# Score matmuls split around an mm1, one PSUM tile per bank and finer filling products in a recurrent attention with a cosine feed-forward layer

## The chip, the cores and the metric

The kernel runs on one core of a Trainium2 chip. The metric is the device time of one execution in microseconds (us), the median of several runs of the same program. The engines are TensorE (PE, with its weight loads listed as PEld), VectorE (DVE), ScalarE (ACT), GpSimd (POOL) and SyncE (SP), which here issues nearly all DMAs.

## The reference

Two parts follow each other: an attention with a decaying state, and a feed-forward layer whose gate is h*cos(h).

```
for t in range(S):                       # B=4, H=8, S=768, D=48
    cur = einsum('bhd,bhe->bhde', u[None] * kt, vt)
    y[:, :, t] = einsum('bhd,bhde->bhe', rt, state + cur)
    state = wt[:, :, :, None] * state + einsum('bhd,bhe->bhde', kt, vt)

x = y.transpose(0, 2, 1, 3).reshape(B * S, H * D)    # 3072 x 384
h = x @ w_in                                          # w_in 384 x 2048
g = h * cos(h)
out = g @ w_out                                       # w_out 2048 x 384
```

## The kernel before, in words

**Tiling.** The 3072 tokens are 24 chunks of 128; two chunks (`BLK`) make a block of 256 tokens, and there are 12 blocks. The hidden size 2048 is cut into 8 units of 256 for each block. A unit is one `mm1` (18 matmuls of 128x256, L594), a gate, and one `mm2` (12 matmuls of 128x384, L612). The factors are split into a high and a low fp32r part and multiplied in three passes (`PASSES`), so 18 is 2 tiles x 3 contractions x 3 passes. The gate of a unit has six steps: I (ACT, L557) and S (DVE, L560) reduce the argument, N (ACT, L573) is the sine, M (DVE, L574) multiplies by h, H (ACT) makes the high part `gs`, L (POOL) the low part. `mm2` of a unit is issued two units after its `mm1` (`LAG`). `mm1` writes its result `ph` into one of two PSUM banks in turn, so `mm1` of a unit writes the bank whose last reader is M of two units before.

**Attention of a chunk.** It is made one block ahead of its use, in small steps that stand between the gate's steps: e and f are scans that make the decays (L283, L289), r and k scale the factors (L300, L302), `lr`, `m`, `u`, `c` and A make `asb`, a tile with the bonus term on its diagonal (A on POOL, L335). `a` (function `att_scores`, L382) computes the scores of the chunk with 16 matmuls into two PSUM banks `pa`, and P (L396) places them into `asb` with six predicated copies on DVE. `t` turns the keys with 16 DMA transposes into `top0` or `top1` (L425, on SP), K brings them from there into `kn` (DVE, L429). `o`, `p` and `s` (matmuls into `py` and `pst`, L479 to L513 and L444) use `asb`, the state and `kn` to make the output and the next state; d makes the decayed state `dd` (DVE, L358).

**What sets the order.** The engines PE, DVE, ACT and POOL run their instructions in the order in which the program is written. `START` orders the first two blocks by hand, `FIRST` the third, and the eight rows of `PLAN`, one for each unit, the blocks after it; `LAST` is the end. In a row, `a+2` is step a of the chunk two after the block's first one, and the names I S N M mm2 H L are those of the unit itself, in the order of their issue; `up` (called by the rows) issues `mm1` and `mm2`. The order of SP's queue is made by a scheduler from when its DMAs' data are made and freed.

**Banks.** `bank(kind, shape, name)` takes the next PSUM bank of a kind by turns from `BANKS[stage]`; from the end of `START` (stage 3) kind a, for `pa`, `py`, `pst`, has the four banks a0, a1, a2, h2, and kind h, for `ph`, has h0 and h1. Each call makes a new tile there, and the program waits, at a tile's first use, until the one before it in that bank is done with.

**Filling products.** D in `START` (handled in `at_first`, L740) issues matmuls of the identity with itself into a bank that nobody reads, while PE has nothing else to do.

Of the kernel before, what the change touches and what calls it, by code (L numbers as in the profile page):

```python
# [10 lines left out]
F32 = mybir.dt.float32  # L11
# [11 lines left out]
C = 128  # L23
# [34 lines left out]
PLAN = ["mm1 I S k+3 N M mm2 H L f+3",  # L58
# [7 lines left out]
START = """  # L66
ld0 e0 f0 ld1 raw2 raw1 q0 e1 k0 D3 pc0 r0 q1 cd0 v0 v1 raw0 f1 D3 a0 W0 wg2 wl2 A0 k1 pc1 wl1 r1 wy2 P0 cd1 D1 a1
wc2 t0 wg1 A1 ld3 ld2 wg0 W1 t1 P1 v5 wx2 wy1 o0 K0 K1 xh0.0 xp0.0 s0 wl0 e3 q3 wc1 xa0.0 wy0 wc0 xh0.1 wp1 f3 pc3
xp0.1 wv1 wx0 xa0.1 q2 e2 n0 k3 f2 raw3 k2 m0.0 m1.0 pc2 t3 r3 I0 r2 wg3 raw4 v2 wl3 cd2 v3 raw5 wy3 m0.1 cd3 S0 t2 a3
A3 K3 K2 A2 P3 ld7 wl4 wg4 a2 ld5 wc3 wg5 N0 raw8 raw6 P2 s1 wx3 raw9 n1 o1 xh1.0 xl1.0 raw7 lr5 v4 ld4 m1.1 xh1.1  # L70
# [26 lines left out]
def rwkv_cos_ffn(ctx: ExitStack, tc: tile.TileContext, tr, tn, tv, u, ut, wts, w, rkw, vst, us, xs, out):  # L97
    nc = tc.nc
# [12 lines left out]
    ps = fast.enter_context(tc.tile_pool(name="ps", bufs=1, space=bass.MemoryType.PSUM))  # L111
    turn = {"a": 0, "h": 0}

    def bank(kind, shape, name):

        tags = BANKS[stage[0]]
        turn[kind] += 1
        return ps.tile(shape, F32, tag=tags[kind][turn[kind] % len(tags[kind])], name=name)

    stage = [0]  # L120

    def buf(tag, shape, dtype, name=None, pool=sb):
        return pool.tile(shape, dtype, tag=tag, name=name or tag, bufs=BUFS.get(tag, 1))
    ident = cst.tile([C, C], F32, name="ident")
# [51 lines left out]
    def fetch_weights(f):  # L176

        place = NF + 1 - RING + (f - 1) % RING
        raw[f] = wt.tile([128, 4 * DM], I32, tag=f"w{place}", name="raw")
        E["qf"].dma_start(out=raw[f].bitcast(I16)[:, :8 * DM - 1], in_=wts[f, :, 1:])  # L180
# [55 lines left out]
    def chunk(j):  # L236

        if j not in atts:
            atts[j] = {"j": j, "g": order[j], "b": order[j] // NCB, "c": order[j] % NCB}
        return atts[j]  # L240

    def att_load(j):
        a = chunk(j)
        g = a["g"]
        a["tt"] = tt = buf("tt", [C, TRW], F32)
        half = 1024 + NP // 2 * 129
        for cols in (*(((half, TRW), (1024, half)) if not atts_loaded else ((1024, TRW),)), (512, 1024), (0, 512)) if j < IN_PARTS else ((0, TRW),):
            E["qt"].dma_start(out=tt[:, slice(*cols)], in_=tr[g, :, slice(*cols)])  # L248
        a["tt"] = tt = tt[:R]
        a["r3"] = tt[:, 0:512].rearrange("p (a t) -> p a t", a=NP)  # L250
        a["k3"] = tt[:, 512:1024].rearrange("p (a t) -> p a t", a=NP)
        a["halves"] = not atts_loaded
        atts_loaded.append(j)
        if j == 0:
            E["qt"].dma_start(out=u_by_head, in_=ut)
# [51 lines left out]
    def att_diag(a):  # L307
        if a["j"] < BY_PE:
            pc = bank("a", [C, 512], "pc")[:, :8]
            for p in range(NP):  # L310
                nc.tensor.matmul(out=pc[:, 2 * p:2 * p + 2], lhsT=a["rkt"][:, p], rhs=u_by_head[:, p], start=True, stop=True)

            def sums():
                a["cd"] = buf("cd", [C, 8], F32)
                copy("cd", a["cd"], pc)

            part(("cd", a["j"]), sums)
        else:
            rk = a["rk"][:, 0]
            part(("m", a["j"]), lambda: E["rk"].tensor_tensor(out=rk, in0=rk, in1=a["rk"][:, 1], op=ALU.mult))  # L320
            part(("u", a["j"]), lambda: E["ru"].tensor_tensor(out=rk, in0=rk, in1=told["u"], op=ALU.mult))

            def sums():
                a["cd"] = buf("cd", [C, 8], F32)
                nc.vector.tensor_reduce(out=a["cd"], in_=rk.rearrange("p (h d) -> p h d", d=HD), axis=mybir.AxisListType.X, op=ALU.add)  # L325

            part(("c", a["j"]), sums)
        part(("A", a["j"]), lambda: picked(a))
# [22 lines left out]
    def att_dstate(a):  # L351

        if a["c"] == 0:
            return

        def decayed():
            a["dd"] = buf("dd", [R, NP, HD], F32)
            E["dd"].tensor_tensor(out=a["dd"], in0=states[a["b"]], in1=a["ee"][:, :, 0:1].to_broadcast([R, NP, HD]), op=ALU.mult)  # L358

        def placed():  # L360
            a["past"] = past[a["j"] % BLK]
            for h in range(2):
                copy("pc%d" % h, a["past"][rows(h), :, h * HD:(h + 1) * HD], a["dd"][rows(h)])

        part(("d", a["j"]), decayed)
        part(("pp", a["j"]), placed)
# [215 lines left out]
    def mm1(t, half=None):  # L582
        i, u = seq[t]
        if not half:
            for j in range(BLK):
                att(i * BLK + j, "x")
            units[t] = bank("h", [C, FU, BT], "ph")
        xT, ph = xts[i], units[t]
        for fi in range(FU) if half is None else (half,):
            steps_of = [(kt, a, b) for kt in range(KT) for a, b in PASSES]  # L590
            if half is not None:
                steps_of.sort(key=lambda x: (x[1], x[2]))
            for n, (kt, a, b) in enumerate(steps_of):
                nc.tensor.matmul(out=ph[:, fi], lhsT=wgt[u * FU + fi][:, 0, a, kt * 128:(kt + 1) * 128], rhs=xT[:, b, kt],  # L594
                                 start=n == 0, stop=n == 3 * KT - 1)
        if half is None or half == FU - 1:
            gate(sb, ph, t)
# [40 lines left out]
    for i in PAIR:  # L638
# [7 lines left out]
                 a=att_scores, t=att_transpose, s=att_state, o=att_own, p=att_past, x=att_x)  # L646
# [64 lines left out]
    def at_first(token):  # L711

        by = re.match(r"(W|H|wc)([av])(\d+)$", token)
        if by:
            name = dict(W="whole", H="gh", wc="whi0")[by[1]]
            usual, E[name] = E[name], dict(a=nc.scalar, v=nc.vector)[by[2]]
            parts.pop((by[1], int(by[3])))()
            E[name] = usual
            return
        if token[:2] == "wp":  # L720
            parts.pop(("wx", int(token[2:])))
        if token[:2] == "wx":
            for x in "wp", "wv":
                parts.pop((x, int(token[2:])))
        if token[:2] == "xp":
            parts.pop(("xl", (int(token[2]), int(token[4]))))
        if token[:2] == "xl":
            for x in "xp", "xa":
                parts.pop((x, (int(token[2]), int(token[4]))))
        n, at, side = re.match(r"(mm2\.|m[01]\.|[a-zA-Z]+)(\d+)(?:\.(\d))?$", token).groups()  # L730
        j = int(at)
        if n == "ld":
            att_load(j)
            att_decay(atts[j])
            seen.update({(j, "load"), (j, "decay"), (j, "x")})
        elif n == "D":
            tags = BANKS[stage[0]]["h"]
            filled = ps.tile([C, 4, C], F32, tag=tags[(turn["h"] + 1) % len(tags)], name="filled")
            for again in range(j):
                nc.tensor.matmul(out=filled, lhsT=ident, rhs=ident.unsqueeze(1).to_broadcast([C, 4, C]), start=True, stop=True)  # L740
        elif n == "raw":
            fetch_weights(j)
            load_weights(j)
        elif n in ("v", "lr"):
            steps[{"v": "lv", "lr": "lr"}[n]](chunk(j))
            seen.add((j, {"v": "lv", "lr": "lr"}[n]))
            if n == "lr":
                att_diag(chunk(j))
                seen.add((j, "diag"))
        elif n == "pc":  # L750
            att_diag(atts[j])
            seen.add((j, "diag"))
        elif n in ("a", "t"):
            steps[n](atts[j])
            seen.add((j, n))
        elif n in ("o", "p", "s"):
            steps[n](j)
            seen.add((j, n))
            if n == "o" and atts[j * BLK]["c"] == 0:
                att_past(j)  # L760
                seen.add((j, "p"))
        elif n in ("m0.", "m1."):
            mm1(j, int(n[1]))
        elif n == "mm2.":
            mm2(j)
        else:
            if n == "d":
                att_dstate(atts[j])
                seen.add((j, "d"))
            parts.pop((n, (j, int(side)) if side else j))()  # L770
            if n == "A" and j == ALL_OF - 1:
                nc.gpsimd.tensor_copy(out=turned_mask, in_=mask)
                nc.gpsimd.memset(turned_mask[:ROW, TURNED:, ROW:], 0)
                nc.gpsimd.memset(turned_mask[ROW:, TURNED:, :ROW], 1)
# [219 lines left out]
```

## Time and profile before

| | before |
|---|---|
| median of 3 runs | 497.48 us |
| lowest and highest run | 496.69, 498.38 us |
| the profiled execution, its own time | 497.93 us |
| its span | 496.1 us |
| mean granted TensorE clock | 0.998 |
| PE busy | 487.1 us |
| PEld busy | 466.8 us |
| DVE busy | 393.2 us |
| ACT busy | 257.8 us |
| POOL busy | 218.0 us |

The span is what the profiler saw of one execution, from the first to the last instruction; the execution's own time lies around it. Busy times are sums over an engine's instructions; weight loads overlap matmuls. In the chain and the waits, "issue" is time in which an engine waited for nothing that the profile shows. A matmul of fp32 factors is two records in the trace, so the 16 score matmuls of a chunk are 32 records, the scores of a block 64, and a filling product is two.

### The profile page before, as it was taken

The numbers are of one execution on the slowest core, as the hardware profiler recorded it, in microseconds if no ns is written. First come the engines' busy times: TensorE is split into PE (matmuls) and PEld (weight loads), VectorE is DVE, ScalarE is ACT, GpSimd is POOL, SyncE is SP. The second block draws the span as 40 slices with busy tenths as digits, with TensorE's granted clock in tenths as the row PEclk, the third lists the DMA queues.
The fourth block names the chain that finished last, engine by engine and source line by source line (L and its number), as shares of the span: only waits on it lengthen the run. The fifth ranks groups of instructions, "written<-read, shape, count | busy, mean of one in ns | idle before, by whom it ended". The sixth has DMA issues, their size and how long they took to land.

```text
span 496.1 us, 13443 instructions
## 1 busy us (share of the span) xinstructions
PE 487.1 (98%) x5514; PEld 466.8 (94%) x5514; DVE 393.2 (79%) x681; ACT 257.8 (52%) x444; POOL 218.0 (44%) x280
## 2 busy tenths in 40 slices
PE   8999999999999999999999999999999999999996
PEld 4689999999999999999999999999999999999996
DVE  7999899898979779769968958967966967587632
ACT  3899988435445445444445345345435445544542
POOL 5138798344436236234435343534624533432330
PEclk9999999999999999999999999999999999999999
DMA  8998830234444152153152150242223212023001
GB/s 275 416 400 296 345 107 6 49 110 130 125 127 158 20 199 80 18 199 77 19 201 49 45 191 22 80 120 96 75 67 133 65 32 97 33 68 127 32 2 36
DMA packets 46289, 58.59 MB, mean 118 GB/s; under 512 B 30736, under 2 KB 37392, under 8 KB 46224
## 3 DMA queue, kind: packets, MB, share of 16 engines
q1 hardware_dynamic: 46080, 57.59, 35.4%
q8 instruction: 45, 0.74, 0.6%
q14 instruction: 20, 0.16, 0.1%
q10 hardware_dynamic: 144, 0.10, 0.1%
HBM read 49.80 MB, written 4.72 MB: 110 GB/s over the span
## 4 chain that ended last, share of the span: by engine, by line
PE 89%; DVE 4%; DMA 2%; ACT 2%; SPq 1%; issue 1%; POOL 0%; DVEq 0%
PE ph L594 40%; PE acc L612 38%; PE pa L382 3%; PE py L479 2%; PE py L485 2%; DMA raw<-wts 2%; PE py L513 1%; PE pst L444 1%; DVE h L203 1%; PE py L507 1%; DVE rr L560 1%; DVE w L205 1%; SPq L248 1%; DMA rk<-tt 0%; PE pa L374 0%
## 5 line engine op out<-in xcount | busy, mean ns | idle before, releaser
L174 POOL TENSOR_TENSOR gs<-rr,gs 128x256 fp32r<-128x256 f32 x188 | 160.8, 876 | 217.9 <-ACT gs L171 209.7
L594 PE MATMUL ph<-xT,w 128*128 128x256 f32 x1728 | 219.7, 281 | 0.8 <-DVE rr L574 0.6
L594 PEld LDWEIGHTS ph<-xT,w 128*128 128x128 f32 x1728 | 212.3, 188 | 4.8 <-PE py L513 1.8
L612 PE MATMUL acc<-w,gs 128*128 128x384 f32 x1152 | 215.3, 337 | 0.1
L612 PEld LDWEIGHTS acc<-w,gs 128*128 128x128 f32 x1152 | 196.3, 188 | 0.7 <-ACT ob L626 0.4
L573 ACT ACTIVATE rr<-rr,quarter 128x512 f32<-128x512 f32 x96 | 69.5, 724 | 94.2 <-DVE rr L560 94.0
L560 DVE SCALAR_TENSOR_TENSOR rr<-rr,ph 128x512 f32<-128x512 int32 x96 | 65.5, 682 | 45.5 <-ACT rr L557 44.8
L171 ACT CAST gs<-rr 128x512 fp32r<-128x512 f32 x92 | 57.1, 621 | 69.0 <-DVE rr L574 48.9
L574 DVE TENSOR_TENSOR rr<-rr,ph 128x512 f32<-128x512 f32 x96 | 65.1, 679 | 21.8 <-ACT rr L573 19.4
L557 ACT ACTIVATE rr<-ph 128x512 int32<-128x512 f32 x96 | 57.1, 595 | 39.2 <-PE ph L594 38.7
L335 POOL TENSOR_SCALAR_AFFINE_SELECT asb<-cd 128x512 f32<-128x512 f32 x48 | 35.4, 762 | 45.4 <-DVE cd L325 27.0
L396 DVE COPY_PREDICATED asb<-turned_mask,pa 64x128 f32<-64x128 uint8 (+1 forms) x108 | 33.6, 346 | 2.1 <-POOL asb L335 0.3
L283 DVE TENSOR_TENSOR_SCAN ee<-tt,one_e 112x516 f32<-112x516 f32 (+1 forms) x25 | 32.7, 1312 | 1.9 <-DMA tt<-tr 1.9
L289 DVE TENSOR_TENSOR_SCAN tt<-tt,inj 112x516 f32<-112x516 f32 x24 | 30.3, 1261 | 0.8
L174 DVE TENSOR_TENSOR xT<-py,xT 128x384 fp32r<-128x384 f32 x22 | 11.3, 550 | 17.4 <-ACT xT L171 17.4
L195 ACT ACTIVATE top<-raw 128x768 f16<-128x768 bf16 x16 | 17.3, 1088 | 3.8 <-DMA raw<-wts 3.0
L479 PE MATMUL py<-asb,v 128*32 128x128 f32 x384 | 18.0, 276 | 0.3 <-DVE asb L393 0.2
L485 PE MATMUL py<-asb,v 128*32 128x128 f32 x384 | 17.3, 273 | 0.0
L171 ACT CAST xT<-py 128x384 fp32r<-128x384 f32 x24 | 10.5, 482 | 12.6 <-PE py L513 8.4
L203 DVE CUSTOM_DVE_ANT_0 h<-h,top 128x1536 uint16<-128x1536 uint16 x16 | 16.3, 1021 | 0.5 <-ACT h L191 0.5
L171 ACT COPY past<-dd 48x192 f32<-48x192 f32 x40 | 14.0, 349 | 2.7 <-DVE dd L358 2.4
L382 PEld LDWEIGHTS pa<-tt 48*64 48x64 f32 x576 | 12.9, 134 | 2.2 <-issue 2.2
(94 smaller groups left out, 352.9 us busy)
## 6 DMA issues: line engine op xcount, KB each, us to landing
tt<-tr SPq DMA_DIRECT2D x22, 770.5 KB, 7.0
raw<-wts SPq DMA_DIRECT2D x16, 767.8 KB, 6.6
rk<-tn SPq DMA_DIRECT2D x20, 384.0 KB, 4.2
v<-tv SPq DMA_DIRECT2D x24, 224.0 KB, 4.5
ww<-w SPq DMA_DIRECT2D x6, 768.0 KB, 5.3
out<-ob SPq DMA_DIRECT2D x23, 192.0 KB, 2.0
top<-tt SPq DMA_DIRECT2D x112, 16.0 KB, 1.9
top<-tt SPq DMA_DIRECT2D x112, 8.0 KB, 1.8
```

What stands on the lines that cost most here:

```text
L171: (nc.scalar.copy if E[name] is nc.scalar else E[name].tensor_copy)(out=out, in_=in_)
L174: E[name].tensor_tensor(out=out, in0=full, in1=high.bitcast(F32), op=ALU.subtract)
L283: nc.vector.tensor_tensor_scan(out=ee[:, pairs].rearrange("p a t -> p (a t)")[:, ::-1], data0=wp[:, cols][:, ::-1], data1=one_e[:, pairs]. ...
L289: nc.vector.tensor_tensor_scan(out=wp[:, 0:W129], data0=wp[:, 0:W129], data1=inj.rearrange("p a t -> p (a t)"), initial=0.0, op0=ALU.mult, ...
L335: nc.gpsimd.affine_select(out=asb, in_=col.unsqueeze(2).to_broadcast([C, NP, C]), pattern=[[0, 4], [1, C]], compare_op=ALU.is_equal, fill= ...
L396: nc.vector.copy_predicated(*(which(x) for x in (a["asb", h], turned_mask, pa[h])))
L557: nc.scalar.activation(made["rr"].bitcast(I32), ph, AF.Copy, scale=INV2PI / W_SCALE, bias=0.25)
L560: nc.vector.scalar_tensor_tensor(out=made["rr"], in0=made["rr"].bitcast(I32), scalar=-2.0 * math.pi * W_SCALE, in1=ph, op0=ALU.mult, op1=A ...
L573: N=lambda: nc.scalar.activation(made["rr"], made["rr"], AF.Sin, scale=1.0 / W_SCALE, bias=quarter),
L574: M=lambda: nc.vector.tensor_tensor(out=made["rr"], in0=made["rr"], in1=ph, op=ALU.mult), H=high, L=low)
L594: nc.tensor.matmul(out=ph[:, fi], lhsT=wgt[u * FU + fi][:, 0, a, kt * 128:(kt + 1) * 128], rhs=xT[:, b, kt], start=n == 0, stop=n == 3 * K ...
L612: nc.tensor.matmul(out=accs[i][j][:, :DM], lhsT=gs[:, a, fi, j * C:(j + 1) * C], rhs=wgt[u * FU + fi][:, 1, b], start=u == 0 and fi == 0 a ...
```

## The change

There are three parts.

- `bank` makes, in stage 3, one tile of 128x512 for each PSUM bank at its first use and gives out slices of it afterwards, where it made a new tile at each call.
- Two rows of `PLAN` change. Steps a+2 and a+3 (the scores) and P+2 and P+3 (their placing) go from the row of unit 4 to that of unit 3, with a+2 ahead of that unit's `mm1` and a+3 behind it; r+4 goes behind S of unit 3; K+2 and m+4 follow in unit 4's row. `FIRST` stays.
- D3, D3 and D1 become D12, D9 and D6, and one filling product has 128 columns instead of 512.

```diff
--- before.py
+++ after.py
@@ -58,13 +58,13 @@
 PLAN = ["mm1 I S k+3 N M mm2 H L f+3",
         "mm1 I S r+3 N M mm2 H L u+3 c+3 lr+5 t+3",
         "load+6 mm1 e+4 I S k+4 N M mm2 H L f+4",
-        "mm1 I S r+4 K+2 N M mm2 H L d+3",
-        "a+2 a+3 mm1 P+2 P+3 I S m+4 N M mm2 H L K+3",
+        "a+2 mm1 a+3 P+2 P+3 I S r+4 N M mm2 H L d+3",
+        "mm1 I S m+4 K+2 N M mm2 H L K+3",
         "mm1 I S u+4 t+4 N M mm2 H L",
         "o+1 p+1 s+1 mm1 load+7 lv+6 lv+7 X+1 n+1 I S c+4 N M mm2 H L d+4",
         "mm1 I S m+5 N M mm2 H L e+5 lr+6"]
 START = """
-ld0 e0 f0 ld1 raw2 raw1 q0 e1 k0 D3 pc0 r0 q1 cd0 v0 v1 raw0 f1 D3 a0 W0 wg2 wl2 A0 k1 pc1 wl1 r1 wy2 P0 cd1 D1 a1
+ld0 e0 f0 ld1 raw2 raw1 q0 e1 k0 D12 pc0 r0 q1 cd0 v0 v1 raw0 f1 D9 a0 W0 wg2 wl2 A0 k1 pc1 wl1 r1 wy2 P0 cd1 D6 a1
 wc2 t0 wg1 A1 ld3 ld2 wg0 W1 t1 P1 v5 wx2 wy1 o0 K0 K1 xh0.0 xp0.0 s0 wl0 e3 q3 wc1 xa0.0 wy0 wc0 xh0.1 wp1 f3 pc3
 xp0.1 wv1 wx0 xa0.1 q2 e2 n0 k3 f2 raw3 k2 m0.0 m1.0 pc2 t3 r3 I0 r2 wg3 raw4 v2 wl3 cd2 v3 raw5 wy3 m0.1 cd3 S0 t2 a3
 A3 K3 K2 A2 P3 ld7 wl4 wg4 a2 ld5 wc3 wg5 N0 raw8 raw6 P2 s1 wx3 raw9 n1 o1 xh1.0 xl1.0 raw7 lr5 v4 ld4 m1.1 xh1.1
@@ -115,9 +115,17 @@
 
         tags = BANKS[stage[0]]
         turn[kind] += 1
-        return ps.tile(shape, F32, tag=tags[kind][turn[kind] % len(tags[kind])], name=name)
+        tag = tags[kind][turn[kind] % len(tags[kind])]
+        if stage[0] < 3:
+            return ps.tile(shape, F32, tag=tag, name=name)
+        if tag not in whole_banks:
+            whole_banks[tag] = ps.tile([C, 512], F32, tag=tag, name="bank_" + tag)
+        flat = whole_banks[tag][:, :math.prod(shape[1:])]
+        sizes = dict(zip("abc", shape[1:]))
+        return flat.rearrange("p (%s) -> p %s" % ((" ".join(sizes),) * 2), **sizes) if len(sizes) > 1 else flat
 
     stage = [0]
+    whole_banks = {}
 
     def buf(tag, shape, dtype, name=None, pool=sb):
         return pool.tile(shape, dtype, tag=tag, name=name or tag, bufs=BUFS.get(tag, 1))
@@ -735,9 +743,9 @@
             seen.update({(j, "load"), (j, "decay"), (j, "x")})
         elif n == "D":
             tags = BANKS[stage[0]]["h"]
-            filled = ps.tile([C, 4, C], F32, tag=tags[(turn["h"] + 1) % len(tags)], name="filled")
+            filled = ps.tile([C, C], F32, tag=tags[(turn["h"] + 1) % len(tags)], name="filled")
             for again in range(j):
-                nc.tensor.matmul(out=filled, lhsT=ident, rhs=ident.unsqueeze(1).to_broadcast([C, 4, C]), start=True, stop=True)
+                nc.tensor.matmul(out=filled, lhsT=ident, rhs=ident, start=True, stop=True)
         elif n == "raw":
             fetch_weights(j)
             load_weights(j)
```

(`D3`, `D3`, `D1` stand in the first line of `START`.) Eight lines are added ahead of `att_load`, so line n of the functions after `bank` is line n + 8 in the changed kernel: L382 becomes L390, L396 L404, L594 L602.

On PE, the scores of a block before, between mm2 (`acc`) and mm1 (`ph`):

```order
L612 MATMUL acc<-w_459,gs 128x384
L382 MATMUL pa<-tt 64x128 [waits DMAHW1_49]
L382 MATMUL pa<-tt 64x128 x3
L382 MATMUL pa<-tt 64x64 x4
L382 MATMUL pa<-tt 64x128 x4
L382 MATMUL pa<-tt 64x64 x4
L382 MATMUL pa<-tt 64x128 [waits DMAHW0_49]
L382 MATMUL pa<-tt 64x128 x3
L382 MATMUL pa<-tt 64x64 x4
L594 MATMUL ph<-xT,w_844 128x256 [waits DVE_49,PE_49]
```

And the end of the first chunk's scores, mm1 of unit 3 and the start of the second chunk's scores after the change (`bank_a_` and `bank_h_` are whole banks; the number is the tile's):

```order
L390 MATMUL bank_h_1748<-tt 64x64
L390 MATMUL bank_a_1729<-tt 64x64
L602 MATMUL bank_h_1675<-xT,w_719 128x256 [waits DVE_49]
L602 MATMUL bank_h_1675<-xT,w_719 128x256 x8
L602 MATMUL bank_h_1675<-xT,w_802 128x256 x9
L390 MATMUL bank_a_1730<-tt 64x128 [waits DMAHW4_49]
L390 MATMUL bank_a_1747<-tt 64x128
```

One group of scores has become two with an mm1 between them, and the first instruction of that mm1 no longer waits on PE's own counter.

On DVE, the same block from the scan of f+4 on, before (L560 is S, L300 and L302 r+4, L429 K+2, L574 M, L396 P):

```order
L289 SCALAR_TENSOR_TENSOR tt<-tt,inj 112x516
L560 SCALAR_TENSOR_TENSOR rr<-rr,ph 128x512
L300 TENSOR_TENSOR tt<-tt 112x256
L302 TENSOR_TENSOR tt<-tt 112x256
L429 STREAM_TRANSPOSE kn<-top_99 128x512
L574 TENSOR_TENSOR rr<-rr,ph 128x512
L358 TENSOR_TENSOR dd<-all_states,ee 112x192
L396 COPY_PREDICATED asb<-turned_mask,pa 128x2x2x64
L396 COPY_PREDICATED asb<-turned_mask,pa 64x2x64 x2
```

And after, from the last operations of P on:

```order
L404 COPY_PREDICATED asb<-turned_mask,bank_a_1747 64x2x64 x2
L568 SCALAR_TENSOR_TENSOR rr<-rr,bank_h_1675 128x512
L308 TENSOR_TENSOR tt<-tt 112x256
L310 TENSOR_TENSOR tt<-tt 112x256
L582 TENSOR_TENSOR rr<-rr,bank_h_1675 128x512
L366 TENSOR_TENSOR dd<-all_states,ee 112x192
L568 SCALAR_TENSOR_TENSOR rr<-rr,bank_h_1619 128x512
L328 TENSOR_TENSOR rk<-rk 128x384
L437 STREAM_TRANSPOSE kn<-top_99 128x512
L582 TENSOR_TENSOR rr<-rr,bank_h_1619 128x512
```

P's twelve operations now stand directly behind the scan, ahead of S of unit 3, and K+2 stands ahead of M of unit 4 instead of M of unit 3.

## Rows read from the trace of the kernel before

**Rows 1.** The page's first part: busy us (share of the span) xinstructions.

```profile
PE 487.1 (98%) x5514; PEld 466.8 (94%) x5514; DVE 393.2 (79%) x681; ACT 257.8 (52%) x444; POOL 218.0 (44%) x280
```

**Rows 2.** Windows: window, length, busy by engine, granted PE clock, DMA share, GB/s.

```profile
320.00:480.00 160.00, 160.00 (x1781) 156.44 (x1780) 114.88 (x206) 74.76 (x129) 60.14 (x83) 1.00 0.22 74
```

**Rows 3.** PE's and PEld's waits, 160 to 480 us: total, times, longest.

```profile
PE py L513 <- issue: 0.4, 1, 0.4
...
PEld py L479 <- issue: 2.0, 8, 0.2
PEld pa L382 <- issue: 1.7, 7, 0.2
```

**Rows 4.** The chain from 230 to 247 us: start, us, what.

```profile
237.12 1.50 PE pa L382 x64
238.62 2.30 PE ph L594 x18
240.92 2.09 PE acc L612 x12
243.02 2.10 PE ph L594 x18
```

**Rows 5.** The chain inside the scores, two windows from 237.4 us.

```profile
237.39 0.42 PE pa L382 x17
...
237.39 0.76 PE pa L382 x33
```

**Rows 6.** The chain in the start, behind the scores at 84.5 us.

```profile
85.64 4.38 PE acc L612 x24
```

**Rows 7.** DVE's timeline, 230 to 250 us: start, us, line, operation.

```profile
230.54 1.64 DVE L283 TENSOR_TENSOR_SCAN ee<-tt,one_e 112x516 f32<-112x516 f32 x1
...
236.29 0.69 DVE L560 SCALAR_TENSOR_TENSOR rr<-rr,ph 128x512 f32<-128x512 int32 x1
236.90 0.93 DVE L300 TENSOR_TENSOR tt<-tt 112x256 f32<-112x256 f32 x1
...
238.09 0.70 DVE L429 STREAM_TRANSPOSE kn<-top 128x512 f32<-128x512 f32 x1
238.72 0.64 DVE L574 TENSOR_TENSOR rr<-rr,ph 128x512 f32<-128x512 f32 x1
...
239.56 3.92 DVE L396 COPY_PREDICATED asb<-turned_mask,pa 128x256 f32<-128x256 uint8 x12
```

**Rows 8.** POOL's timeline in that block.

```profile
232.67 1.41 POOL L335 TENSOR_SCALAR_AFFINE_SELECT asb<-cd 128x512 f32<-128x512 f32 x2
```

**Rows 9.** ACT's timeline in that block.

```profile
237.01 0.72 ACT L573 ACTIVATE rr<-rr,quarter 128x512 f32<-128x512 f32 x1 [0.82 <-DVE rr L560]
```

**Rows 10.** DVE's timeline in two other blocks: S(3), behind the scan.

```profile
159.23 0.69 DVE L560 SCALAR_TENSOR_TENSOR rr<-rr,ph 128x512 f32<-128x512 int32 x1
...
393.39 0.69 DVE L560 SCALAR_TENSOR_TENSOR rr<-rr,ph 128x512 f32<-128x512 int32 x1
```

**Rows 11.** The chain in these two blocks: mm1 of unit 5.

```profile
164.98 2.10 PE ph L594 x18
...
399.77 2.10 PE ph L594 x18
```

**Rows 12.** SP's queue, 238.5 to 255 us: start, us, DMAs issued.

```profile
238.81 11.06 SPq L425 DMA_DIRECT2D top<-tt  x16
```

**Rows 13.** The page's DMA issues, and its costliest groups: a weight load.

```profile
tt<-tr SPq DMA_DIRECT2D x22, 770.5 KB, 7.0
...
L594 PEld LDWEIGHTS ph<-xT,w 128*128 128x128 f32 x1728 | 212.3, 188 | 4.8 <-PE py L513 1.8
```

**Rows 14.** PE's timeline in the start: filling products.

```profile
7.61 2.82 PE L740 MATMUL filled<-ident 128*128 128x512 f32 x6
...
12.79 1.10 PE L740 MATMUL filled<-ident 128*128 128x512 f32 x2
```

**Rows 15.** The chain in the start: the placing.

```profile
15.90 1.36 DVE asb L393 x2
```

## The prediction

> **What bounds the kernel now.** I read the page's busy totals first, then the windows, PE's waits, the chain's pieces in a block, and last the timelines of the other engines there. In the totals the reader is to see that TensorE (PE) is busy 487.1 us of a span of 496.1 and VectorE (DVE) 393.2 [rows 1]. [...] Among PE's waits from 160 to 480 us there is one, of 0.4 us, on "issue"; the weight loads (PEld) idle 0.24 us ahead of each group of small matmuls, on "issue" again [rows 3]. So nothing that another engine does holds PE up where the change is: a wait removed there cost nothing, and the time is the sum of what PE has to do. Two questions remain: how long PE's new order takes by itself, and whether an engine that is early enough now comes too late.
>
> **What a group of scores costs.** In a block of some 39.0 us the pieces of the chain from 237.12 us are: the small score matmuls of two chunks (32 instructions, two records each) in 1.50 us, the 18 of mm1 behind them in 2.30, 12 of mm2 in 2.09, and an mm1 that follows mm2 in 2.10 [rows 4]. Inside the score group, 17 records take 0.42 us and 33 take 0.76 [rows 5], so 16 take 0.34 and 64 take 1.36. The group is 0.14 us longer than its records, the mm1 behind it 0.20 longer than one behind mm2. A visit to the small tiles thus costs **0.34 us** beyond its records, however many these are: 0.14 at the way in, 0.20 at the way out. One group in the start stands between mm1 and mm2, as the second half of the split will: the 24 matmuls of mm2 behind it take 4.38 us, against 2 x 2.09 = 4.18 [rows 4, 6], so the way out is 0.20 there too. The way in from mm1 is the one part that no row prices.
>
> **PLAN, the split of the scores.** Before, both chunks' scores stand between mm2 and mm1 of unit 4. After, one chunk's 32 records stand ahead of mm1 of unit 3 and the other's 32 behind it, ahead of mm2. The matmuls are the same; a block has two visits instead of one. Eight blocks have the row: 8 x 0.34 = 2.7 us, all on PE, on the path. Bounds: nothing, if the second visit is hidden; 8 x (0.24 + 0.20) = 3.5, if PEld's idle time [rows 3] counts whole at the way in. I take **+2.8**, near the 0.34, both ends of which were seen.
>
> [...]
>
> **PLAN, the moves on DVE.** P (the placing, 12 operations, 3.92 us) goes ahead of S of unit 3, the r+4 scaling behind it, K+2 one unit later. In the trace the scan of f+4 gives way to S(3) at 236.29 [rows 7]. I lay the new order from there. The scores are done at about 236.9 for P's second half, the masks' tiles since about 234.1 [rows 8]. P runs 236.3 to 240.2, S(3) to 240.85, r+4 (1.19 between starts) to 242.05; ScalarE's N(3), 0.72 [rows 9], is through by 241.7; M(3), 0.64, ends at 242.7. Who waits: mm1 of unit 5 writes the bank that M(3) frees. It starts at 243.02 now [rows 4], at 243.37 behind the second visit. **Slack 0.7 us**, where M(3) now ends 3.7 us ahead [rows 7]. The same sum of 6.4 us from the end of the scan, in the other blocks: 1.1 us left in three of them and 0.7 in one more. The block at 393 us has 0.3 (393.39 + 6.4 against 399.77 + 0.35), the last one has no scan and more room. In the first block changed the scan gives way at 159.23, later against PE than elsewhere, and mm1 of unit 5 starts at 164.98: M(3) ends at 165.6, against 165.33 [rows 10, 11]. There PE waits 0.3 us and the semaphore's way: **+0.4**, once. Behind that, K+2 and M(4) end near 247.0 and K+3 near 247.8; mm1 of unit 6 and the state matmuls that read them stand behind unit 5 and the matmuls of py.
>
> **PLAN, the moves on SP's queue.** The 16 transposes into top0 wait for K+2, which reads top0. They now start at 238.81, as K+2 ends, and take 11.06 us; v, tt and rk stand behind them [rows 12]. With K+2 at about 245.8 to 246.4 they move by 7.6 us, to 257.5, and the loads to 257.5 to 261. A load of tt is 7.0 us under way [rows 13], so it lands near 266; the scan e+4 of the next block, which reads it, starts 39.0 us after 230.54 [rows 7], at 269.5. Cover 3.5 us, cost 0.
>
> **Whole-bank tiles.** One tile per bank turns the wait at a tile's first use into waits by regions; PE's instructions that wait on PE's own counter go from 135 to 34. No such wait shows in the trace [rows 3]. At most the gap of 0.4 us goes, and the idle time ahead of pa and py, 3.7 us, if tiles cause it. I take -0.1. A false wait between two users of a bank is covered by the slack above.
>
> **Filling products.** The seven are six, six and two records; the second six take 2.82 us, the two 1.10 [rows 14]. By columns, 12 of 128 equal three of 512, nine are three quarters of three, six are one and a half of one. The first filling keeps its length. The second shrinks to 2.1, and PE then waits for DVE's tt, as now. The third grows by 0.5, and the second scores end near 15.6; the chain there runs over POOL's asb and DVE's placing, begun at 15.90 [rows 15], so it is hidden. Cost 0. If a record of 128 columns took 0.30 (0.19 of weight load [rows 13] and 0.11 of columns), the second filling would end 2.2 later, the third 2.5, and about +2 would show.
>
> **The sum.** 2.8 + 0.4 - 0.1 = 3.1. The profiled execution has 497.93 us, 496.1 of span and 1.83 around it, 0.45 above the median of 497.48. From its own time the sum gives 501.0, from the median **500.6 us**. Times are told apart here by about 0.3%, 1.5 us.
>
> **Rivals.**
> - *The second visit is mostly hidden*: 0 to 1.2 us in all, 497.5 to 498.7, no difference. For it, the way in from mm1 is unpriced, and PEld is ahead of PE there. Against it, 0.20 at the way out both times. 0.20.
> - *DVE becomes the bound* at mm1 of unit 5. It decides where M(3) is later than laid by over 0.3 to 1.1 us, block by block. If P waits for the last scores (0.6) and N(3) is served 0.5 late, M(3) is 1.1 late: 1.1 more in the first block, 0.8 at 393 us, 0.4 in two: +2.7, 503.3. Against it, every duration is the block's own. 0.08.
> - *The start or SP's queue costs* up to 2 more, 502.6: 0.07.
> - *Faster*: the idle time ahead of pa and py, 2.0 + 1.7 us [rows 3], is the tile's release, which the whole-bank tiles make unneeded, and the gap of 0.4 goes too. [...] For it, these groups are where a fresh tile is taken. Against it, mm1 and mm2 change tiles without such idle time, and the way out, which no tile explains, is as large. It decides once pa's way in falls under 0.05 us. 0.10.
> - That PE's order does not change is excluded by the order of its instructions.
>
> **How the numbers follow.** The forecast, 500.6 with its own range of 499.6 to 501.6, has 0.55; hidden 0.20, faster 0.10, DVE 0.08, start or queue 0.07. From 497.8 to 502.0 lie the forecast, most of the hidden case and half of the start's, 0.8 in all. Slower by over 1.5 us, above 499.0: 0.55 + 0.08 + 0.07 = 0.70. Within: 0.20. Faster: 0.10.
>
> **What would show it.** The new chain should have two pieces of 32 score records in a block, of some 0.8 us each, with 2.3 for the mm1 behind the first and 2.3 for the mm2 behind the second, and a block of 39.35 us. PE should have one wait for DVE (M, the multiplication by ph) near 165 us and none later; P should start as the f+4 scan ends, and top0's transposes 7.6 us later. I am wrong if the pieces of 32 take under 0.7 us or mm2 behind them 2.1 (a visit is cheaper), if PE waits for M in most blocks (DVE bounds it), or if the blocks keep their length and the start changed.

## The result, and the profile after

| | before | after |
|---|---|---|
| median | 497.25 us (6 runs) | 500.17 us (6 runs) |
| lowest and highest run | 496.37, 498.38 us | 499.06, 501.11 us |
| the profiled execution: its time, its span | 497.93, 496.1 us | 499.06, 497.2 us |

The ratio of after to before is 1.0059, with a 95% interval of 1.0043 to 1.0075: the changed kernel is slower by 2.9 us (2.1 to 3.7). The two profiled executions lie only 1.13 us apart, since the one of after was the fastest of its six runs and the one of before was above its median. So the change is not read from the spans, but from a block.

The chain of the changed kernel, from 230 to 250 us. The pieces of the second chunk's scores are printed one by one, because the two banks alternate; they run from 236.12 to 236.95:

```profile
232.99 0.83 PE bank_a L390 x32
233.82 2.30 PE bank_h L602 x18
236.12 0.25 PE bank_h L390
...
236.95 2.31 PE acc L620 x12
...
243.44 2.10 PE bank_h L602 x18
```

Against [rows 4] the reader is to see two visits of 0.83 us where one of 1.50 was: 0.16 more at the way in. The first visit is followed by an mm1 of 2.30, the second by an mm2 of 2.31 where 2.09 is usual: 0.22 more at the way out. That is 0.38 a block. The output copies on ACT, one for each block, give the length of a whole block; first two rows of before, then two of after:

```profile
307.51 0.85 ACT L626 ACTIVATE ob<-acc 128x384 f32<-128x384 f32 x2
346.51 0.85 ACT L626 ACTIVATE ob<-acc 128x384 f32<-128x384 f32 x2
```

```profile
307.55 0.85 ACT L634 ACTIVATE ob<-acc 128x384 f32<-128x384 f32 x2
346.91 0.85 ACT L634 ACTIVATE ob<-acc 128x384 f32<-128x384 f32 x2
```

A block has 39.00 us before and 39.36 after. Eight blocks of 0.36 to 0.37 more make 2.9 to 3.0 us, which is the whole of the measured difference.

From 160 to 480 us the changed kernel's PE has no wait in the profile at all. PEld's waits there are:

```profile
PEld bank_h L602 <- issue: 1.6, 8, 0.2
PEld bank_a L390 <- issue: 1.2, 5, 0.2
PEld bank_a L487 <- issue: 1.2, 5, 0.2
...
PEld bank_h L390 <- issue: 0.5, 2, 0.2
...
PEld bank_h L602 <- DVE rr L582: 0.2, 1, 0.2
```

PE's gap of 0.4 us on "issue" [rows 3] is not there in this execution. The idle time of 0.25 ahead of the score loads is, but in only 7 of the 14 score groups of this stretch (L390: five listed under bank_a, two under bank_h). These seven are the groups behind mm2. Ahead of the seven behind mm1 PEld idles about half as long, too briefly to be listed; in the block at 233 us it is 0.13 us, from the end of mm1's loads at 235.92 to 236.05:

```profile
233.75 2.17 PEld L602 LDWEIGHTS bank_h<-xT,w 128*128 128x128 f32 x18
236.05 0.13 PEld L390 LDWEIGHTS bank_h<-tt 48*64 48x64 f32 x1
```

Both kinds of group take 0.83 us in the chain all the same, so PEld's idle time is not what a visit costs. The last row of the waits is the one wait for M that was forecast, at 164 us; it stands on PEld and not on PE. The chain has an mm1 of 2.24 there instead of 2.10:

```profile
164.34 2.24 PE bank_h L602 x18
```

DVE's timeline and SP's queue in the block of [rows 7]:

```profile
234.65 1.23 DVE L297 TENSOR_TENSOR_SCAN tt<-tt,inj 112x516 f32<-112x516 f32 x1
235.80 1.88 DVE L404 COPY_PREDICATED asb<-turned_mask,bank_a 128x256 f32<-128x256 uint8 x6
...
239.62 0.69 DVE L568 SCALAR_TENSOR_TENSOR rr<-rr,bank_h 128x512 f32<-128x512 int32 x1
240.23 0.42 DVE L308 TENSOR_TENSOR tt<-tt 112x256 f32<-112x256 f32 x1
240.56 0.42 DVE L310 TENSOR_TENSOR tt<-tt 112x256 f32<-112x256 f32 x1
241.11 0.69 DVE L582 TENSOR_TENSOR rr<-rr,bank_h 128x512 f32<-128x512 f32 x1
...
244.87 0.71 DVE L437 STREAM_TRANSPOSE kn<-top 128x512 f32<-128x512 f32 x1
```

```profile
233.92 23.04 SPq L433 DMA_DIRECT2D top<-tt  x22
257.06 0.53 SPq L256 DMA_DIRECT2D tt<-tr  x1
```

P starts as the scan ends. M(3) ends at 241.80, and mm1 of unit 5 starts at 243.44: 1.6 us of room. K+2 is done at 245.6, top0's transposes run to 256.96, and the load of tt follows at 257.06. The scan e+4 that needs it started at 269.97, without a wait.

### The profile page after: what moved, and what is told of

Same layout as the page of the kernel before. It is cut to its first block, busy times and chain, and to the rows that moved or that the text cites. A ratio compares the mean times of both kernels' runs of the same rounds, so it can differ in the third digit from the quotient of the medians.

```text
span 497.2 us, 13421 instructions
## 1 busy us (share of the span) xinstructions
PE 489.6 (98%) x5554; PEld 473.5 (95%) x5554; DVE 388.9 (78%) x681; ACT 258.4 (52%) x444; POOL 215.6 (43%) x280
## 4 chain that ended last, share of the span: by engine, by line
PE 87%; DVE 8%; ACT 2%; issue 1%; DMA 1%; SPq 0%; DVEq 0%
PE acc L620 38%; PE bank_h L602 34%; PE ph L602 4%; PE bank_a L390 2%; DVE h L211 2%; PE bank_a L487 1%; DVE w L213 1%; PE bank_a L493 1%; DVE ee L291 1%; DVE rr L582 1%; PE bank_a L452 1%; ACT w L179 1%; PE bank_h L390 1%; PE bank_a L521 1%; DVE rr L568 1%
## 5 line engine op out<-in xcount | busy, mean ns | idle before, releaser
L602 PE MATMUL bank_h<-xT,w 128*128 128x256 f32 x1404 | 178.6, 281 | 0.0
L602 PEld LDWEIGHTS bank_h<-xT,w 128*128 128x128 f32 x1404 | 173.0, 188 | 2.7 <-issue 1.8
L568 DVE SCALAR_TENSOR_TENSOR rr<-rr,bank_h 128x512 f32<-128x512 int32 x78 | 53.3, 683 | 54.6 <-ACT rr L565 54.0
L582 DVE TENSOR_TENSOR rr<-rr,bank_h 128x512 f32<-128x512 f32 x78 | 53.2, 682 | 20.4 <-ACT rr L581 17.2
L565 ACT ACTIVATE rr<-bank_h 128x512 int32<-128x512 f32 x78 | 46.7, 599 | 36.8 <-PE bank_h L602 35.6
L602 PE MATMUL ph<-xT,w 128*128 128x256 f32 x324 | 41.3, 282 | 0.9 <-DVE rr L582 0.6
L602 PEld LDWEIGHTS ph<-xT,w 128*128 128x128 f32 x324 | 39.4, 188 | 2.3 <-PE acc L620 0.9
L404 DVE COPY_PREDICATED asb<-turned_mask,bank_a 64x128 f32<-64x128 uint8 (+1 forms) x81 | 25.0, 344 | 2.2 <-PE bank_a L390 1.2
L211 DVE CUSTOM_DVE_ANT_0 h<-h,top 128x1536 uint16<-128x1536 uint16 x16 | 16.4, 1022 | 0.6 <-ACT h L199 0.6
L390 PE MATMUL bank_a<-tt 48*64 48x128 f32 (+1 forms) x432 | 15.9, 250 | 0.0
L390 PEld LDWEIGHTS bank_a<-tt 48*64 48x64 f32 x432 | 13.5, 133 | 2.3 <-issue 1.5
```

The costliest lines, as they stand in the source:

```text
L390: nc.tensor.matmul(out=pa[h][keys, at, cols], lhsT=a["k3"][rows(h), at, keys], rhs=a["r3"][rows(h), at, cols], start=True, stop=True)
L565: nc.scalar.activation(made["rr"].bitcast(I32), ph, AF.Copy, scale=INV2PI / W_SCALE, bias=0.25)
L568: nc.vector.scalar_tensor_tensor(out=made["rr"], in0=made["rr"].bitcast(I32), scalar=-2.0 * math.pi * W_SCALE, in1=ph, op0=ALU.mult, op1=A ...
L582: M=lambda: nc.vector.tensor_tensor(out=made["rr"], in0=made["rr"], in1=ph, op=ALU.mult), H=high, L=low)
```

## The experiments

Theory: the time is PE's second visit to the small tiles, 0.36 to 0.37 us in each of eight blocks, and nothing else. Rivals: a part comes from the whole-bank tiles, from the filling products, or from DVE's and SP's new order.

### The three parts of the change, each alone

The two new rows of PLAN in the kernel before:

```diff
-"mm1 I S r+4 K+2 N M mm2 H L d+3", "a+2 a+3 mm1 P+2 P+3 I S m+4 N M mm2 H L K+3"
+"a+2 mm1 a+3 P+2 P+3 I S r+4 N M mm2 H L d+3", "mm1 I S m+4 K+2 N M mm2 H L K+3"
```

> The kernel before with the two new rows of PLAN alone; a new tile at each call of bank and the seven filling products of 512 columns stay. Theory (the second visit to the small tiles costs PE 0.37 us in each of 8 blocks): 2.9 us over the kernel before, about 500.2, with two score pieces of 0.83 us in a block, 2.30 for the mm1 and 2.31 for the mm2 behind them. Rival (the whole-bank tiles cost a part): clearly under 2.9, say 1 to 2. Rival (the filling products cost it): 0 to 1.

Measured: 500.10 us against 496.99, ratio 1.0065 (1.0047 to 1.0082). Its chain has the pieces of the changed kernel:

```profile
233.22 0.83 PE pa L382 x32
234.04 2.30 PE ph L594 x18
236.34 0.83 PE pa L382 x32
237.17 2.31 PE acc L612 x12
```

These two rows make the whole difference by themselves.

Whole-bank tiles in the kernel before:

```diff
-        return ps.tile(shape, F32, tag=tags[kind][turn[kind] % len(tags[kind])], name=name)
+        tag = tags[kind][turn[kind] % len(tags[kind])]
...
+        if tag not in whole_banks:
+            whole_banks[tag] = ps.tile([C, 512], F32, tag=tag, name="bank_" + tag)
+        flat = whole_banks[tag][:, :math.prod(shape[1:])]
...
```

> The kernel before with whole-bank tiles alone. Theory: no difference, within 0.7 us of the kernel before, a block of 39.0 us, the score group 1.50 us and the mm1 behind it 2.30. Rival (waits at a tile's first use cost PE something that shows as idle time ahead of the small groups): faster by 1 to 3.7 us, with less than 0.14 us at the way in. Rival (the tiles cost): slower by 1 to 3.

Measured: 497.18 us against 496.99, ratio 1.0009 (0.9997 to 1.0022), no difference. PEld still idles ahead of the small groups:

```profile
PEld bank_a L390 <- issue: 1.0, 4, 0.2
PEld bank_a L487 <- DVE rr L568: 1.0, 4, 0.2
```

What is named there has changed for some groups, and the length of 0.25 us has not: that idle time is not the tile's release. The rival that ended on the faster side falls with this.

The 27 filling products of 128 columns in the kernel before:

```diff
-D3 ... D3 ... D1        (seven of 512 columns)
+D12 ... D9 ... D6       (27 of 128)
```

> The kernel before with the 27 filling products of 128 columns alone. Theory: within 0.7 us of the kernel before; the blocks unchanged at 39.0 us. Rival (the filling products cost or gain in the start): 1 to 2 us either way, all of it ahead of 108 us.

Measured: 498.81 us against 496.99, ratio 1.0033 (1.0020 to 1.0046). This was not expected: 1.8 us slower by the medians (1.0 to 2.3 by the interval). The start is not later: the first output copies on ACT stand at 107.00 us here, and at 108.38 in the kernel before. PE's waits name another place:

```profile
PE py L513 <- issue: 1.4, 2, 0.8
```

In the chain these are gaps among the past matmuls (L513, on the state that is kept in `past`), the last small ones of the visit for py:

```profile
171.07 0.59 PE py L513 x30
171.66 0.83 issue
172.49 0.38 PE py L513 x2
...
328.31 0.36 PE py L513 x10
328.67 0.56 issue
329.23 0.63 PE py L513 x22
```

These 32 records take 0.60 us where there is no gap, so they are longer by 1.20 and 0.95 us here, and by 0.75 at the one gap of the kernel before. That is 1.4 us more, of the 1.8 of the medians. But it is one execution of each, and these two are only 0.3 us apart in their whole time (498.25 and 497.93), so the cause of the 1.8 is not shown.

The DMA view from 169 to 170 us, shortly ahead of the first gap, has one transfer of the instruction queue:

```profile
q8 instruction: 1, 0.02, 7.8%
```

The gap of [rows 3] in the kernel before is of the same kind: "issue", in the past matmuls, behind an instruction transfer. Such a transfer does not tell a visit with a gap from one without, though: behind 120 us, seven of the nine visits for py in the kernel before have one that begins inside the visit, and one of the seven has the gap. At 328.05 us, for example, one begins in the visit of 325.9 to 329.6, which has none.

### Does the number of filling products move these gaps?

```diff
-D12 ... D9 ... D6       (27 of 128 columns)
+D8 ... D6 ... D4        (18 of 192 columns)
```

> The kernel before with 18 filling products of 192 columns (8, 6 and 4): the columns of the change's 27 of 128, with 11 more instructions on PE than before instead of 20. The change's filling products alone took 1.6 us with no later start: their trace shows PE standing 1.1 and 0.8 us in the past matmuls of two blocks, on issue, with an instruction transfer just ahead of each. [...] Rival (fewer filling columns cost the time itself): again 1.6 over, with stalls in the same two blocks.

Measured: 499.87 us against 496.63, ratio 1.0075 (1.0060 to 1.0090): slower still, by 3.2 us, outside what was expected. (The expectation's 1.1 and 0.8 us are not what the profile shows: PE's idle times were 0.83 and 0.56, and the past matmuls were longer by 1.20 and 0.95.) PE waits twice on "issue", 1.3 us in all. The larger gap has moved from 171 us to 133; the smaller one stands behind 320 us, where PE is busy for 159.66 us of 160, so 0.34; with 27 products the smaller one stood at 329:

```profile
132.90 0.56 PE py L513 x21
133.45 1.00 issue
134.46 0.44 PE py L513 x11
```

A second difference is in the start. PE stood idle for 0.60 us ahead of the first scores, and the granted clock from 12 to 20 us is 0.79 where before and after have 1.00:

```profile
10.10 1.16 PE L374 MATMUL pa<-tt 48*128 48x128 f32 x16 [0.60 <-DVE tt L298]
...
14.50 1.85 PE L374 MATMUL pa<-tt 48*128 48x128 f32 x16
```

```profile
12.00:20.00 8.00, 7.64 (x110) 6.49 (x113) 6.86 (x11) 6.00 (x10) 1.79 (x3) 0.79 1.03 420
```

The second scores take 1.85 us instead of the 1.16 of the first. So this kernel is no clean trial of the number of instructions: it moved one gap, still had a second, and its clock was lower in the start as well. That 18 or 27 products are worse than seven in the kernel before is measured. That the instruction transfers make the gaps is a guess: they stand in visits without a gap too, and no run takes them away.

### The early placing without the split

The changed kernel with one visit a block, everything else as changed:

```diff
-"a+2 mm1 a+3 P+2 P+3 I S r+4 N M mm2 H L d+3"
+"a+2 a+3 mm1 P+2 P+3 I S r+4 N M mm2 H L d+3"
```

> The changed kernel with both chunks' scores together ahead of mm1 of unit 3, so that everything is one unit sooner as in the change but there is one visit a block. Theory: 0 to 0.5 us over the kernel before (one wait of 0.15 us for M in the first block), blocks of 39.0 us, the score group 1.50. Rival (placing one unit sooner makes DVE or SP's queue late): the 2.9 us stay, with waits for M or for tt on PE.

Measured: 497.70 us against 496.99, ratio 1.0023 (1.0005 to 1.0040): 0.7 us over the kernel before by the medians, where the changed kernel is 2.9 over it, and a little more than expected. Whether the rest is from the filling products was tried with the seven old ones:

> The unsplit kernel with the seven filling products of the kernel before: whole-bank tiles, and scores and placing one unit sooner in one group. Theory (the early placing and the tiles are free, and what the unsplit kernel had over the kernel before came from the finer filling products): within 0.5 us of the kernel before, blocks of 39.0 us. Rival (the early placing costs by itself): 0.5 to 1.5 over it, as the unsplit kernel.

Measured: 497.30 us against 496.92, ratio 1.0008 (0.9996 to 1.0020), no difference. Scores and placing one unit sooner, K+2 one later, top0's transposes behind it and whole-bank tiles together cost nothing that the runs can tell. The step from 1.0023 to 1.0008 is smaller than the two intervals, so that the rest came from the filling products is likely and not shown. In the profiled execution PE has one wait for M behind the start, of 0.5 us:

```profile
PE bank_h L602 <- DVE rr L582: 0.5, 1, 0.5
```

They gain nothing either: no version that was tried beats the kernel before.

### The split without the early placing, and the visits in other places

The kernel before with one token moved:

```diff
-"a+2 a+3 mm1 P+2 P+3 I S m+4 N M mm2 H L K+3"
+"a+2 mm1 a+3 P+2 P+3 I S m+4 N M mm2 H L K+3"
```

> The kernel before with one token moved: a+3 stands behind mm1 of unit 4 instead of ahead of it; nothing goes a unit sooner, DVE's and SP's orders, the banks and the filling products stay. Theory (the second visit alone makes the time): blocks of 39.37 us, 2.9 us over the kernel before, 499.9. Rival (DVE's or SP's new order makes part of it): under 2.

Measured: 500.04 us against 496.63, ratio 1.0064 (1.0049 to 1.0079). Its output copies, again two blocks:

```profile
309.05 0.85 ACT L626 ACTIVATE ob<-acc 128x384 f32<-128x384 f32 x2
348.41 0.85 ACT L626 ACTIVATE ob<-acc 128x384 f32<-128x384 f32 x2
```

39.36 us again. The 3.4 us of the medians are 2.4 to 3.9 by the interval, which holds the 2.9 of the whole change. One token in one of the eight rows makes the change in time.

Both visits between mm2 and mm1, in units 3 and 4:

```diff
-"a+2 mm1 a+3 P+2 P+3 I S r+4 N M mm2 H L d+3", "mm1 I S m+4 K+2 N M mm2 H L K+3"
+"a+2 mm1 P+2 I S r+4 N M mm2 H L d+3", "a+3 mm1 P+3 I S m+4 K+2 N M mm2 H L K+3"
```

> The changed kernel with a+3 moved on to the place ahead of mm1 of unit 4, so that both visits stand between mm2 and mm1, and P+3 goes with it. Theory (a visit costs 0.14 to 0.15 at the way in and 0.20 to 0.22 at the way out, wherever it stands): blocks of 39.35 to 39.37 us, 2.8 to 3.0 over the kernel before, as the change. Rival (the cost comes from standing between mm1 and mm2): under 1.5.

Measured: 499.47 us against 496.63, ratio 1.0080 (1.0052 to 1.0107). One of its four runs, at 502.81 with a mean granted clock of 0.991, pulls the ratio up; by the medians it is 2.84 us. The chain has 0.83 and 2.30 twice in a block. It did not matter between which matmuls the second visit stood: 2.84 us here, 2.9 with the change.

### What a visit costs, by itself

Four kernels add one matmul of 64 columns ahead of mm1 of units 1, 3 and 5, 27 in all, into columns of an acc bank that are not read. The weights are 48x64 or 128x128, fp32 or fp32r:

```diff
+        if half is None and t >= 24 and t % NU in (1, 3, 5):
+            spare = accs[seq[t - 3][0]][0][0:64, DM:DM + 64]
+            nc.tensor.matmul(out=spare, lhsT=ident[0:48, 0:64], rhs=ident[0:48, 0:64], start=False, stop=True, skip_group_check=True)
```

> The kernel before with one matmul more ahead of mm1 of units 1, 3 and 5 of the blocks from the third on, 27 in all: weights of 48x64 of fp32, 64 columns, into columns of an acc bank that nobody reads. It is a visit to the small tiles of two records, as small as can be. Theory (a visit costs 0.34 to 0.37 beyond its records, however many): 27 x (0.35 + 0.04) = 10.5 us over the kernel before, with mm1 behind a probe 2.30 instead of 2.10. Rival (the cost grows with the records): under 3 us.

> The same 27 matmuls in the same places, fp32, but with weights of 128x128. Theory (it is the change of the tile's size that costs): no visit, the price of two records with their loads, 27 x 0.2 = 5 us at most, mm1 behind it 2.10. Rival (it is fp32 between fp32r that costs, or any small matmul that stands alone): 0.35 a visit and its records, 10 us or more, mm1 behind it 2.30.

> The same 27 with weights of 48x64 and 64 columns of fp32r, one record each. Theory (the tile's size): about as in fp32, 27 x 0.35 = 9.5 us, mm1 behind it 2.30. Rival (fp32): 27 x 0.05 = 1 to 2 us, mm1 2.10.

> The same 27 with weights of 128x128 and 64 columns of fp32r: neither the tile's size nor the kind changes. Both theories: only the price of one more weight load and 64 columns, 27 x 0.05 to 0.12 = 1.5 to 3 us, mm1 behind it 2.10. More than that is the price of one more instruction of any kind, and is to be taken off the other three.

Measured, one run each beside 496.79 us of the kernel before: 508.65, 503.24, 507.15 and 501.15. The added matmul (L590) and the mm1 behind it in the four chains, in that order:

```profile
266.52 0.26 PE acc L590 x2
266.77 2.30 PE ph L597 x18
```

```profile
264.84 0.17 PE acc L590 x2
...
273.62 2.17 PE ph L597 x18
```

```profile
265.72 0.17 PE acc L590
265.89 2.30 PE ph L597 x18
```

```profile
263.99 0.03 PE acc L590
264.02 2.18 PE ph L597 x18
```

| | piece | over 2.10 behind it | sum |
|---|---|---|---|
| 48x64, fp32 (two records) | 0.26 | 0.20 | 0.46 |
| 128x128, fp32 (two records) | 0.17 | 0.07 | 0.24 |
| 48x64, fp32r (one record) | 0.17 | 0.20 | 0.37 |
| 128x128, fp32r (one record) | 0.03 | 0.08 | 0.11 |

27 times these sums are 12.4, 6.5, 10.0 and 3.0 us; the single runs gave 11.9, 6.4, 10.4 and 4.4, and a single run can be off by 1 us. The blocks of the four kernels, which have three of the added matmuls each, bear the sums out: from the first mm1 of a block to that of the next they take 40.36, 39.72, 40.10 and 39.34 us against 39.00, so 0.45, 0.24, 0.37 and 0.11 for each matmul. Two records are already a whole visit: the cost does not grow with the records. The way out of 0.20 goes with the tile's size, in fp32 and fp32r alike, and 0.07 to 0.08 of it is paid by the two lone matmuls of full size too. The size costs 0.22 in fp32 and 0.26 in fp32r; fp32 between fp32r costs 0.09 to 0.13, one more record included. The theory of the tile's size holds for the larger part, not for all of it. The expectation for the full-size fp32 matmul had mm1 behind it at 2.10 and the chain shows 2.17.

## Why the prediction was right

**The split.** It was forecast at 2.8 us, eight second visits of 0.35, and is 0.36 to 0.37 a block. The way out at 0.20 was read rightly from both sorts of places [rows 4, 6]; the way in from mm1, which no row priced, is as large as the way in from mm2: both pieces take 0.83 us, 0.15 more than 32 records at the rate of [rows 5]. The split alone gives 500.04 us, and the change without the split loses its cost, so this is shown from both sides.

The prediction's bound of 3.5 us took PEld's idle time as a measure of the way in. That was not sound: ahead of the second visit PEld idles 0.13 us instead of 0.25, and the visit costs the same. What excludes a hidden way in is the length of the blocks: with it hidden, the eight second visits would have cost 8 x 0.20 = 1.6 us, by the way out alone, and the blocks are longer by 0.36 to 0.37 each, 2.9 to 3.0 in all.

The four added matmuls put 0.22 to 0.26 us on the change of the tile's size, there and back. What PE does in that time no run shows.

**DVE.** The wait for M in the first block is there, once, with 0.14 us instead of 0.4. The 0.1 that the forecast had there for the semaphore's way is shown by no run; M ends at 164.16 us after the change, and PEld starts the first load of the mm1 that waits for it at 164.21, 0.05 us later. The step that was mis-sized is the r+4 scaling: it was laid with 1.19 us between starts and takes 0.88 in its new place, two operations of 0.42. In the kernel before, its first half took 0.93 [rows 7]. P also started 0.5 us earlier than laid, and the slack in the block at 230 us is 1.6 us, not 0.7. How long the wait is differs between kernels and executions: 0.5 us in the unsplit kernel with the old filling products, and in the unsplit one with the finer ones an mm1 of 2.18, that is 0.08. The rival that DVE becomes the bound did not come near.

**SP's queue.** Top0's transposes end at 256.96 (laid at 257.5), the loads behind them land in time: cost 0, as forecast.

**Whole-bank tiles.** -0.1 forecast, no difference measured. The gap of 0.4 us is not there with the tiles alone, nor with PLAN's rows alone, and both unsplit kernels, which have these tiles, have one, of 0.3 and 0.2 us.

**Filling products.** Here the forecast of 0 was wrong for the part alone: 1.8 us (1.0 to 2.3 by the interval), and not by the mechanism that the upper bound of +2 priced, since the start is not later and a record of 128 columns takes 0.13 us and not 0.30 (second and third filling after the change):

```profile
7.91 2.25 PE L748 MATMUL filled<-ident 128*128 128x128 f32 x18
12.10 1.58 PE L748 MATMUL filled<-ident 128*128 128x128 f32 x12
```

So the work in the start was priced rightly: the second filling takes 2.25 where 2.1 was laid, the third is 0.48 longer where 0.5 was. What the forecast left out shows, as far as the profile goes, in the gaps at 171 and 328 us. In the change the 1.8 does not come on top: PLAN's rows alone give 1.0065 and the whole change 1.0059. That the total came out right owes something to this, which nothing in the prediction foresaw. What makes the gaps, and how often each kernel has them, stays open: a profile shows one execution.

**The rivals.** "The second visit is mostly hidden" and "faster" are excluded by the blocks of 39.36 us. The sum of 3.1 us met 2.9 (2.1 to 3.7): the split came 0.15 dearer, the wait for M 0.26 cheaper, and the tiles gave nothing where 0.1 was taken off, so the terms as measured add up to 3.1 again. Of the way from 500.6 to 500.17, 0.23 is the kernel before, whose median is 497.25 with more runs, not 497.48; the other 0.2 is within the interval.

## What to carry to other kernels

On an engine that is busy all the time, count the visits: a group of small matmuls between large ones had a price here that did not grow with its length, 0.34 us beyond its records with 64 of them, 0.36 for each more of 32, 0.37 in all with a single one. So two chunks' groups belong together, and one token that splits them can be dearer than everything else in a change. Price such a step from the pieces ahead of and behind the group in the chain, less its records at their own rate. The idle time of the weight loads ahead of such a group is not that price: it was 0.25 us in one place and 0.13 in the other, for the same cost. PE's waits on its own counter showed nowhere in the profile, and without most of them the kernel took 497.18 us against 496.99: see first whether a wait shows.

## What was not expected of the hardware

PE stands 0.2 to 1.0 us in some blocks, among the past matmuls at the end of a visit for py: 0.36 us in the kernel before, 0.83 and 0.56 with 27 filling products, 1.00 and 0.34 with 18. Ahead of three of these gaps the DMA view has an instruction transfer: 2.0 us ahead in the kernel before (287.75 and 289.77), about 1.8 ahead of the first one with 27 products and 1.4 ahead of the first with 18. The instruction queue (q8) moves 0.74 MB in 45 transfers, 16.4 KB each, in before and after alike. That a transfer which comes late makes PE stand is a guess: in the kernel before, six of the nine visits for py behind 120 us have such a transfer inside and no gap.

With 18 filling products PE's clock fell to a granted mean of 0.79 from 12 to 20 us, after an idle time of 0.60 us ahead of the scores. With 0.35 us at that place in the kernel before, and none in the changed one, it was 1.00 from 12 to 20 us. That the idle time made it fall is not shown: no kernel changes it alone.
